# 1e-9 added from a PSUM column, query and key loads two units ahead, first weights converted three units later

## The chip, the cores and the metric

The kernel runs on one core of one Trainium2 chip. The metric is the device time of one execution in microseconds (us). The core has five engines: TensorE (PE in the profile) multiplies matrices into PSUM, VectorE (DVE), ScalarE (ACT) and GpSimd (POOL) work element by element, and SyncE (SP) issues most of the DMAs. Each engine takes its own instructions in order; engines wait for each other by semaphores.

## The reference

Attention with two masks on 8 batches, 8 heads, 576 positions and 64 dimensions, and then a feed-forward layer with 2048 hidden columns:

```python
scores = q @ k^T / sqrt(64)
# heads 0-3: local,   seen where 0 <= row - col < 32
# heads 4-7: strided, seen where col <= row and col % 32 == row % 32
scores = where(mask, scores, -1e9) - max over the row
attn = exp(scores);  attn = attn / (sum(attn) + 1e-9)
x = (attn @ v) as 4608 tokens x 512
h = x @ w_in                # 512 x 2048
out = (h * cos(h)) @ w_out  # 2048 x 512
```

All arrays are fp32 for the user; the weights lie in DRAM as 64-bit numbers.

## The kernel before

**Stages.** The 4608 tokens are 12 blocks of 384. The attention of batches 0 and 1 is done first, alone: this is the opening stage, and all that the change touches. After it the feed-forward layer of blocks 0 and 1 runs, then blocks 2 to 5 with the attention of batches 2 to 7 spread between their steps, then the last six blocks in pairs. From the end of the opening stage on, TensorE has one long list of feed-forward matmuls: `hidden` (L493, the first layer) and `outer` (L519, the second), later L793 and L822. Each fp32 operand is split in a rounded part and a rest (`x_hi`, `x_lo`, and the weights' tiles named `s`).

**Units of the opening stage.** Each batch has seven units of attention, in the order strided, strided, local, strided, strided, local, local: units 0 to 13 for the two batches. A unit goes through these steps:
- SP loads its q and k (tile `qk`, L363 strided, L306 local) and its v (L369, L300).
- TensorE writes the mask into one of three PSUM banks (L239) and adds the scores (L382, L318).
- DVE takes the row maximum (L254) and subtracts it (L255), ACT takes the exponential (L266), DVE sums it (L281), adds 1e-9 (L282, six columns of `z` in SBUF) and takes the reciprocal (L283), and POOL multiplies (L285).
- The result is transposed: strided units by TensorE (L402) and an ACT copy (L406), local ones by DVE (L328).
- TensorE multiplies by v (L416, L347), ACT copies the product out (L424, L430, L355, L356), and ACT and POOL split it in two parts (L447, L448).

**Turns.** A loop over the units (L639) sets the order of TensorE's work by hand; `in_turn` (L200) chains the matmuls. Turn n issues the scores of unit n, then a few *warm matmuls*, then the products of unit n-4, the transposes of unit n-3, and last the softmax of unit n. The warm matmuls (`keep_busy`, L628) multiply a tile of zeros into the PSUM bank `spare` (named `acc2`, rows 0 to 63 of it); nobody uses what they write, they only keep TensorE at work. How many there are is in `BUSY`: 10 ahead of turn 0, then 6, 5, 3, 2, 2, 2 and 1 in each turn after.

**Weights.** `load_weight` (L143) loads a slice f of w_in or w_out (`raw`, L147) and turns it from 64-bit numbers to an fp32 pair: on DVE L161 (for w_out on ACT, L156), L162 and L170, on ACT L169 and L174, on POOL L175. For f = 0 no order to the units was given, and for f = 1 the conversions stand behind the sums (L281) of units 8 and 10 (`SECOND`). A weight's load stands behind the q and k load that `WEIGHTS_AT` names. `need_weights(cv, 1)` is called after the loop (L649), and the other slices follow in the feed-forward steps.

**What else sets the order.** A scheduler orders the instructions of DVE, ACT, POOL and SP within such rules. Where two engines use one PSUM tile, each waits for the other's last use of that tile, whatever columns they use.

Of the kernel before, what the change touches and what calls it, by code (L numbers as in the profile page):

```python
# [19 lines left out]
ALU = mybir.AluOpType  # L20
# [6 lines left out]
P = 128  # L27
# [27 lines left out]

LAG = 3
AHEAD = 2
SECOND = 8, 10
CONVERTED = {3: (1, 0)}

WEIGHTS_AT, WEIGHTS_EACH = 4, 1

PRODUCT_LAG, TRANSPOSE_LAG = 4, 3
BUSY = (10, 6, 5, 3, 2, 2, 2) + 8 * (1,)


KNOTS = ((3, 0), (13, 9), (58, 45))
# [22 lines left out]
def attention_cos_ffn(ctx, tc, qkl, vl, qkvs, w_in, w_out, eye, eye16, mask_l0, mask_l, mask_s, out):  # L90
# [88 lines left out]
    def need_weights(cv, f):  # L179
        nonlocal weights  # L180
        for f in range(weights, f + 1):
            if f < AHEAD:
                after = [summed[n] if f else None for n in SECOND]
            else:
                after = 2 * [reduced[CONVERTED.get(f, (0, f - AHEAD))]]
            load_weight(
                cv, w_in.bitcast(I32)[f], wi_h[f].rearrange("p c n -> p (c n)"),
                wi_l[f].rearrange("p c n -> p (c n)"), after[0], False,
            )
            load_weight(cv, w_out.bitcast(I32)[f], wo_h[f], wo_l[f], after[1], True)  # L190
            weights = f + 1
# [16 lines left out]
    class Attention:  # L208
# [41 lines left out]
        def softmax(self, s, mask, n, w, pn=None):  # L250
            t = self.wk.tile([P, SC], F32, name="t_sb", bufs=3 if self.plain else 2)[:, :n * w].rearrange("p (t w) -> p t w", w=w)
            mx = sm.tile([P, SU], F32, name="mx")
            if self.plain:
                nc.vector.tensor_reduce(out=mx[:, :n], in_=s, op=ALU.max, axis=AX.X)  # L254
                nc.vector.tensor_tensor(  # L255
                    out=t, in0=s, in1=mx[:, :n].unsqueeze(2).broadcast_to([P, n, w]), op=ALU.subtract
                )
            else:
                nc.vector.tensor_tensor(out=t, in0=s, in1=mask, op=ALU.add)
                nc.vector.tensor_reduce(out=mx[:, :n], in_=t, op=ALU.max, axis=AX.X)  # L260
                nc.gpsimd.tensor_tensor(
                    out=t, in0=t, in1=mx[:, :n].unsqueeze(2).broadcast_to([P, n, w]), op=ALU.subtract
                )
            if self.plain:
                e = t
                exps.append(nc.scalar.activation(out=e, in_=t, func=AF.Exp, scale=0.125))  # L266
                if self.copied is not None:
                    order(exps[-1], self.copied, "copies first")
            else:
                e = self.wk.tile([P, SC], F32, name="e_sb", bufs=4)  # L270
                e = e[:, :n * w].rearrange("p (t w) -> p t w", w=w)
                silu = nc.scalar.activation(out=e, in_=t, func=AF.Silu, bias=shift1, scale=0.0625)
                if self.copied is not None:
                    order(silu, self.copied, "copies first")
                nc.scalar.activation(out=t, in_=t, func=AF.Silu, bias=shift2, scale=0.0625)
                nc.vector.scalar_tensor_tensor(
                    out=e, in0=t, scalar=-math.exp(STEP), in1=e, op0=ALU.mult, op1=ALU.add
                )
                nc.scalar.activation(out=e, in_=e, func=AF.Square, scale=math.exp(SHIFT) / STEP)
            z = sm.tile([P, SU], F32, name="z")  # L280
            summed.append(nc.vector.tensor_reduce(out=z[:, :n], in_=e, op=ALU.add, axis=AX.X))  # L281
            nc.vector.tensor_scalar(out=z[:, :n], in0=z[:, :n], scalar1=1e-9, scalar2=None, op0=ALU.add)  # L282
            nc.vector.reciprocal(out=z[:, :n], in_=z[:, :n])  # L283
            pn = e if pn is None else pn
            nc.gpsimd.tensor_tensor(  # L285
                out=pn, in0=e, in1=z[:, :n].unsqueeze(2).broadcast_to([P, n, w]), op=ALU.mult
            )
            return pn
# [7 lines left out]
        def local(self, b, u):  # L296

            def load_v():
                v = self.ld.tile([P, max(VL, VS)], F32, name="v", bufs=5 if self.plain else 3)
                load = nc.sync.dma_start(out=v[:, :VL], in_=vl[b, u])  # L300
                if not self.plain:
                    order(load, tiles[-1], "weights first")
                return v

            qk = self.ld.tile([P, max(QKL, QS + KS)], F32, name="qk")
            loads.append(nc.sync.dma_start(out=qk[:, :QKL], in_=qkl[b, u]))  # L306
            if not self.plain:
                order(loads[-1], tiles[-1], "weights first")
            if self.plain:
                v = load_v()  # L310
            q_t = qk[:, :2 * LQ].rearrange("p (h q) -> p h q", h=2)
            k_t = qk[:, 2 * LQ:QKL].rearrange("p (h k) -> p h k", h=2)
            mask = ml0.rearrange("p (t w) -> p t w", w=KW) if u == 0 else ml.unsqueeze(1).broadcast_to([P, LU, KW])
            s_ps = self.score_bank(mask)

            def score(t, c):
                p, j = divmod(c, 2)
                in_turn(nc.tensor.matmul(  # L318
                    s_ps[quarter_of(c), t * KW:(t + 1) * KW], q_t[half(j), p, QB * t:QB * (t + 1)],
                    k_t[half(j), p, QB * t:QB * t + KW], start=not self.plain, stop=True, skip_group_check=True,  # L320
                ))

            yield [partial(score, t, c) for t in range(LU) for c in range(LH)], "64x32"
            pn = self.softmax(s_ps[:, :LU * KW].rearrange("p (t w) -> p t w", w=KW), mask, LU, KW)

            def turn():
                pt = self.wk.tile([P, LU * KW], F32, name="pt_l")
                nc.vector.transpose(out=pt[:, :LU * KW], in_=pn.rearrange("p t w -> p (t w)"))  # L328
                return pt

            if self.plain:
                pt = turn()
            yield
            if not self.plain:
                pt, v = turn(), load_v()
            v_t = v[:, :VL].rearrange("p (m d) -> p m d", d=D)
            yield
            x_t = [self.wk.tile([P, LQ], F32, name="x_l", bufs=4 if self.plain else 2) for _ in range(2)]
            a_ps = [self.bank(self.products), self.bank(self.transposed)]

            def product(m, c):


                p, j = divmod(c, 2)
                lo, hi = max(m - 1, 0), min(m + 1, LU)
                at = m * KW - QB if m else 0
                in_turn(nc.tensor.matmul(  # L347
                    a_ps[p][half(j), lo * QB:hi * QB], v_t[quarter_of(c), m], pt[quarter_of(c), at:at + (hi - lo) * QB],
                    start=m == turns[0], stop=m == turns[-1], skip_group_check=True,
                ))  # L350


            turns = range(0 if u else 1, LU + 1)
            yield [partial(product, m, c) for m in turns for c in range(LH)], "32x64"
            nc.scalar.copy(out=x_t[1], in_=a_ps[1][:, :LQ])  # L355
            self.copied = nc.scalar.copy(out=x_t[0], in_=a_ps[0][:, :LQ])  # L356
            for p in range(2):
                keep(2 + p, b * S + u * LQ, x_t[p])

        def strided(self, b, p, u):  # L360
# [11 lines left out]
                return v  # L372

            if self.plain:
                v = load_v()
            q_t = qk[:, :QS].rearrange("p (t q) -> p t q", q=GB)
            k_t = qk[:, QS:QS + KS].rearrange("p (t k) -> p t k", k=GB)
            mask = ms.unsqueeze(1).broadcast_to([P, SU, GB])
# [2 lines left out]
            def score(t, i):  # L381
# [6 lines left out]
                partial(score, t, i) for t in range(SU) for i in range(2)  # L388
                if SU * u + t // 2 * 2 + i < NG
            ], "64x64"  # L390
            pn = next(self.pn_s)
            self.softmax(
                s_ps[:, :SU * GB].rearrange("p (t w) -> p t w", w=GB), mask,
# [222 lines left out]
    with ExitStack() as loading:  # L616
        cv = loading.enter_context(tc.tile_pool(name="cv", bufs=3, reuse_waits="tile"))
        with ExitStack() as stack:
# [5 lines left out]
            )  # L624
            units = att.units(0) + att.units(1)
            spare = ps.tile([P, 512], F32, name="acc2")

            def keep_busy(n):  # L628
                for _ in range(n):
                    in_turn(nc.tensor.matmul(  # L630
                        spare[:64], warm, warm.unsqueeze(1).broadcast_to([P, 8, 64]), start=True, stop=True
                    ))

            def run(unit):
# [1 line left out]
                    matmul()  # L636

            keep_busy(BUSY[0])
            for n, unit in enumerate(units):  # L639
                run(unit)  # L640
                if n + 1 < len(BUSY):
                    keep_busy(BUSY[n + 1])
                if n >= PRODUCT_LAG:
                    run(units[n - PRODUCT_LAG])
                    next(units[n - PRODUCT_LAG], None)
                if n >= TRANSPOSE_LAG:
                    next(units[n - TRANSPOSE_LAG])
                next(unit)
# [337 lines left out]
```

## Time and profile before

| | |
|---|---|
| time, median of 3 runs | 917.93 us (916.53 to 918.52) |
| the profiled execution's own time | 917.13 us |
| its span, first to last instruction | 915.3 us |
| mean granted TensorE clock | 0.994 |
| TensorE busy | 898.0 us (98%) |
| DVE, ACT, POOL busy | 524.1, 520.6, 434.2 us |
| opening stage: first score matmul, first `hidden` matmul | 5.82 us, 49.53 us |

How to read it: the profile is of one execution. Rows of the timeline have the start, the busy time, engine and line, the tiles written and read, the form, how often, and in square brackets the idle time of the engine just before with what ended it. PEclk is the clock that TensorE was granted, where 1.00 is full speed; before the first record it is not told. Lines are those of the kernel before, unless the text says that they are of the changed one.

### The profile page before, as it was taken

Reading aid. Unit: us, or ns where it says so; the run is one execution under the profiler, and the core shown is the slowest. Engines: PE = TensorE matmul, PEld = TensorE weight load, DVE = VectorE, ACT = ScalarE, POOL = GpSimd, SP = SyncE. Lnnn points to the kernel's source line nnn. Section 1 sums busy time; section 2 is a strip of 40 time slices with the busy share of each in tenths; the row PEclk is TensorE's granted clock in tenths of the full one; section 3 lists DMA queues with packets and bytes.
Section 4 is the critical chain, followed back from the end, with each engine's and each line's share of the span. In section 5 each row is a group of like instructions: output and inputs, shape, how many; then the busy total and the mean of one; then the engine's idle time right before and its main releaser. Section 6 shows DMA issues by size and latency. Waiting matters only on the chain. (4 is left out here: it accounts for less than half of the span.)

```text
span 915.3 us, 20498 instructions
## 1 busy us (share of the span) xinstructions
PE 898.0 (98%) x7876; PEld 788.2 (86%) x7876; DVE 524.1 (57%) x1018; ACT 520.6 (57%) x1091; POOL 434.2 (47%) x466
## 2 busy tenths in 40 slices
PE   8899999999999999999999999999999999999998
PEld 5589999988888888888888988989998989899987
DVE  5867665446656666666663346556464555544453
ACT  3577776466657665656655445545454545544443
POOL 2756655535665667556745524424433434223231
PEclk9799999999999999999999999999999999999999
DMA  8634325145577867544346855657585655756401
GB/s 305 203 123 158 136 102 183 54 149 169 188 236 264 266 237 229 172 159 152 120 163 192 264 166 184 229 157 233 187 266 190 204 181 186 256 180 196 139 24 69
DMA packets 93408, 166.32 MB, mean 182 GB/s; under 512 B 10752, under 2 KB 34304, under 8 KB 93312
## 3 DMA queue, kind: packets, MB, share of 16 engines
q1 hardware_dynamic: 85248, 157.59, 52.2%
q10 hardware_dynamic: 8064, 7.44, 2.4%
q8 instruction: 62, 1.02, 0.4%
q14 instruction: 34, 0.28, 0.1%
HBM read 125.40 MB, written 39.58 MB: 180 GB/s over the span
## 5 line engine op out<-in xcount | busy, mean ns | idle before, releaser
L808 POOL TENSOR_TENSOR g_lo<-r,g_hi 128x384 fp32r<-128x384 f32 x96 | 99.0, 1031 | 247.9 <-ACT g_hi L807 141.2
L512 POOL TENSOR_TENSOR g_lo<-r,g_hi 128x384 fp32r<-128x384 f32 x94 | 101.4, 1079 | 177.4 <-ACT g_hi L511 99.3
L822 PE MATMUL acc<-s,g_hi 128*128 128x512 f32 x576 | 179.7, 393 | 0.0
L519 PE MATMUL acc<-s,g_hi 128*128 128x512 f32 x564 | 176.2, 396 | 0.0
L519 PEld LDWEIGHTS acc<-s,g_hi 128*128 128x128 f32 x564 | 103.1, 188 | 15.2
L822 PEld LDWEIGHTS acc<-s,g_hi 128*128 128x128 f32 x576 | 106.2, 188 | 10.8
L822 PE MATMUL acc<-s,g_lo 128*128 128x512 f32 x288 | 112.7, 391 | 0.0
L493 PE MATMUL b<-x_hi,s 128*128 128x384 f32 x384 | 108.7, 344 | 1.1 <-POOL s L175 0.8
L802 DVE SCALAR_TENSOR_TENSOR r<-r,h 128x384 f32<-128x384 int32 x96 | 58.2, 607 | 89.4 <-ACT r L801 89.4
L493 PE MATMUL a<-x_hi,s 128*128 128x384 f32 x384 | 108.7, 343 | 0.0
L519 PE MATMUL acc<-s,g_lo 128*128 128x512 f32 x282 | 108.6, 390 | 0.0
L793 PE MATMUL a<-s,s 128*128 128x384 f32 x384 | 83.1, 337 | 0.0
L804 DVE TENSOR_TENSOR r<-r,h 128x384 f32<-128x384 f32 x96 | 69.8, 727 | 22.0 <-ACT r L803 20.7
L803 ACT ACTIVATE r<-r,biases 128x384 f32<-128x384 f32 x96 | 59.2, 617 | 36.7 <-DVE r L802 36.4
L503 ACT ACTIVATE r<-r,biases 128x384 f32<-128x384 f32 x96 | 58.8, 612 | 30.0 <-DVE r L500 28.2
L807 ACT CAST g_hi<-r 128x384 fp32r<-128x384 f32 x96 | 49.2, 512 | 46.0 <-DVE r L804 45.6
L493 PEld LDWEIGHTS b<-x_hi,s 128*128 128x128 f32 x384 | 70.1, 188 | 4.6 <-POOL s L175 1.1
L801 ACT ACTIVATE r<-h 128x384 int32<-128x384 f32 x96 | 50.4, 525 | 39.9 <-DVE h L871 24.5
L793 PEld LDWEIGHTS a<-s,s 128*128 128x128 f32 x384 | 69.4, 188 | 4.2
L493 PEld LDWEIGHTS a<-x_hi,s 128*128 128x128 f32 x384 | 70.2, 188 | 2.6
L511 ACT CAST g_hi<-r 128x384 fp32r<-128x384 f32 x94 | 48.1, 512 | 30.2 <-DVE r L506 27.8
L822 PEld LDWEIGHTS acc<-s,g_lo 128*128 128x128 f32 x288 | 54.1, 188 | 12.4
(149 smaller groups left out, 1774.7 us busy)
## 6 DMA issues: line engine op xcount, KB each, us to landing
s<-wis SPq DMA_DIRECT2D x168, 256.0 KB, 2.9
s<-wos SPq DMA_DIRECT2D x96, 256.0 KB, 3.6
qk<-in_qkvs SPq DMA_DIRECT2D x32, 324.0 KB, 3.7
qk<-in_qkl SPq DMA_DIRECT2D x24, 416.0 KB, 4.2
raw<-in_w_in SPq DMA_DIRECT2D x16, 512.0 KB, 4.2
raw<-in_w_out SPq DMA_DIRECT2D x16, 512.0 KB, 3.4
wos<-s SPq DMA_DIRECT2D x32, 256.0 KB, 4.0
wis<-sr SPq DMA_DIRECT2D x32, 256.0 KB, 2.1
```

The lines of the kernel that those rows point to most:

```text
L493: mm = nc.tensor.matmul(h, w[f][:, c], x[c], start=(i == 0), stop=(i == len(ops) - 1))
L503: sin = nc.scalar.activation(out=r, in_=r, func=AF.Sin, bias=quarter)
L512: chain["rest"] = nc.gpsimd.tensor_tensor(out=g_lo, in0=r, in1=g_hi.bitcast(F32), op=ALU.subtract)
L519: mm = nc.tensor.matmul(acc[t], g[:, ts], w[f], start=(f == 0 and i == 0), stop=(f == NFC - 1 and i == 2))
L793: in_turn(nc.tensor.matmul(bank, w[:, n, c], part, start=start and i == 0, stop=stop and i == len(ops) - 1, skip_group_check=True,))
L801: nc.scalar.activation(out=k, in_=h, func=AF.Copy, scale=1.0 / (2.0 * math.pi), bias=0.25)
L802: nc.vector.scalar_tensor_tensor(out=r, in0=k, scalar=-2.0 * math.pi, in1=h, op0=ALU.mult, op1=ALU.add)
L803: nc.scalar.activation(out=r, in_=r, func=AF.Sin, bias=quarter)
L804: chain["curve"] = nc.vector.tensor_tensor(out=r, in0=r, in1=h, op=ALU.mult)
L807: chain["cast"] = nc.scalar.copy(out=g_hi, in_=r)
L808: chain["rest"] = nc.gpsimd.tensor_tensor(out=g_lo, in0=r, in1=g_hi.bitcast(F32), op=ALU.subtract)
L822: in_turn(nc.tensor.matmul(acc, g[gn][:, ts], w[wn], start=done == 0 and i == 0, stop=done == NFC - 1 and i == 2,))
```

## The change

- **1e-9 from PSUM.** In the opening stage the addition on `z` is no longer a DVE instruction with a constant, but one that adds two tensors: `z` in SBUF and six columns that hold 1e-9. Those columns are columns 448 to 453 of the PSUM bank `spare`, written once by a memset. The warm matmuls write the other 448 columns of the same bank, 448 columns wide in place of 512. Later attention units keep the constant.
- **Loads.** A unit's q and k load is issued two turns ahead of its scores (`LOAD_LEAD`); its v load is issued after its scores. The first weight loads stand behind the q and k load of unit 6 and the following ones (`WEIGHTS_AT` was 4).
- **First weights.** The conversions of w_in and w_out for f = 0 stand behind the sums of units 5 and 6 (`CONVERTED_BEHIND`).
- **Warm matmuls.** 10, then 4, 3, 3, 2, 2, 2 and 1 in each turn after: 34 in place of 38.

```diff
-SECOND = 8, 10
+CONVERTED_BEHIND = ((5, 6), (8, 10))
...
-WEIGHTS_AT, WEIGHTS_EACH = 4, 1
+WEIGHTS_AT, WEIGHTS_EACH = 6, 1
...
-BUSY = (10, 6, 5, 3, 2, 2, 2) + 8 * (1,)
+BUSY = (10, 4, 3, 3, 2, 2, 2) + 8 * (1,)
...
-                after = [summed[n] if f else None for n in SECOND]
+                after = [summed[n] for n in CONVERTED_BEHIND[f]]
...
-            nc.vector.tensor_scalar(out=z[:, :n], in0=z[:, :n], scalar1=1e-9, scalar2=None, op0=ALU.add)
+            if self.plain:
+                nc.vector.tensor_tensor(out=z[:, :n], in0=z[:, :n], in1=self.tiny[:, :n], op=ALU.add)
+            else:
+                nc.vector.tensor_scalar(out=z[:, :n], in0=z[:, :n], scalar1=1e-9, scalar2=None, op0=ALU.add)
...
             if self.plain:
-                v = load_v()
+                yield
...
             yield [partial(score, t, c) for t in range(LU) for c in range(LH)], "64x32"
+            if self.plain:
+                v = load_v()
...
             spare = ps.tile([P, 512], F32, name="acc2")
+            att.tiny = spare[:, 448:448 + SU]
+            nc.vector.memset(att.tiny, 1e-9)
...
-                        spare[:64], warm, warm.unsqueeze(1).broadcast_to([P, 8, 64]), start=True, stop=True
+                        spare[:64, :448], warm, warm.unsqueeze(1).broadcast_to([P, 7, 64]), start=True, stop=True
...
+            for unit in units[:LOAD_LEAD]:
+                next(unit)
             for n, unit in enumerate(units):
+                if n + LOAD_LEAD < len(units):
+                    next(units[n + LOAD_LEAD])
                 run(unit)
```

(The strided units have the same two edits around their v load.) In the changed kernel the addition is L283, the reciprocal L286, the warm matmuls L639, the products L423 and L352, the transposes L409, the scores L387 and L321, ACT's copies L413, L360 and L361, and its casts L454; L161 to L175 and L254 to L281 keep their numbers.

The first place is TensorE's list in turns 6 and 7: the warm matmuls (`acc_215` is the bank `spare`) with what each instruction waits for. Before:

```order
L630 MATMUL acc_215<-warm 64x512
L347 MATMUL acc_515<-pt_l,v 64x64 [waits DVE_49,PE_49]
...
L402 MATMUL acc_547<-ident,pn_s_85 128x128 [waits PE_49,Pool_49]
L402 MATMUL acc_547<-ident,pn_s_85 128x128 x2
L239 LDWEIGHTS ident_69
L239 MATMUL b<-ms,ident_69 128x324
L382 MATMUL b<-qk 54x54 [waits DMAHW4_49]
L382 MATMUL b<-qk 54x54 x11
L630 LDWEIGHTS warm
L630 MATMUL acc_215<-warm 64x512
L416 MATMUL acc_585<-pt,v 64x54 [waits DMAHW3_49,Activation_49]
```

The same stretch in the changed kernel:

```order
L639 MATMUL acc_215<-warm 64x448 [waits DVE_49]
L352 MATMUL acc_514<-pt_l,v 64x64 [waits DMAHW2_49,PE_49]
...
L409 MATMUL acc_546<-ident,pn_s_85 128x128 [waits PE_49,Pool_49]
L409 MATMUL acc_546<-ident,pn_s_85 128x128 x2
L239 LDWEIGHTS ident_69
L239 MATMUL b<-ms,ident_69 128x324
L387 MATMUL b<-qk 54x54 [waits DMAHW2_49]
L387 MATMUL b<-qk 54x54 x11
L639 LDWEIGHTS warm
L639 MATMUL acc_215<-warm 64x448 [waits DVE_49]
L423 MATMUL acc_584<-pt,v 64x54 [waits DMAHW4_49,Activation_49]
```

The matmuls stand in the same order. The first warm matmul of each turn from turn 1 on now waits for DVE: the value that it waits for is that of the addition of the unit before, so in turn 7 that of unit 6.

The second place is ACT's list around the conversions for f = 0 (`t_sb` is a unit's scores, `bits` and `raw` a weight slice). Before, from unit 3's exponential to unit 5's:

```order
L266 ACTIVATE t_sb<-t_sb 128x324 [waits DVE_49]
L156 ACTIVATE bits<-raw 128x512 [waits DMAHW1_49]
L424 COPY x_t<-acc_391 128x6x18x3 [waits PE_49]
L174 CAST s_92<-bits 128x512 [waits DVE_49]
L406 COPY pt<-acc_405 128x324 [waits PE_49]
L266 ACTIVATE t_sb<-t_sb 128x324 [waits DVE_49]
L169 ACTIVATE raw<-raw 128x512 [waits DVE_49]
...
L174 CAST s_124<-bits 128x512 [waits DVE_49]
L266 ACTIVATE t_sb<-t_sb 128x384 [waits DVE_49,Pool_49]
```

The changed kernel, from unit 5's exponential to unit 6's:

```order
L266 ACTIVATE t_sb<-t_sb 128x384 [waits DVE_49,Pool_49]
L454 CAST x_hi<-x_t 128x384 [waits Activation_49]
L454 CAST x_hi<-x_t 128x192
L156 ACTIVATE bits<-raw 128x512 [waits DMAHW3_49]
L169 ACTIVATE raw<-raw 128x512 [waits DMAHW1_49,DVE_49]
L174 CAST s_92<-bits 128x512 [waits DVE_49]
L360 COPY x_l<-acc_515 128x192 [waits PE_49]
L361 COPY x_l<-acc_514 128x192
L454 CAST x_hi<-x_l 128x192 [waits Activation_49]
L454 CAST x_hi<-x_l 128x192
L413 COPY pt<-acc_546 128x324 [waits PE_49]
L266 ACTIVATE t_sb<-t_sb 128x384 [waits Pool_49]
```

The conversion of w_in for f = 0 (L169, and L174 into `s_92`) ended between the exponentials of units 3 and 4 and now stands between those of units 5 and 6; unit 6's exponential is behind its last step.

The third place is the head of SP's list. Before:

```order
L363 DMA qk<-in_qkvs 128x648
L369 DMA v<-in_qkvs 128x384
L363 DMA qk<-in_qkvs 128x648
L369 DMA v<-in_qkvs 128x320
L306 DMA qk<-in_qkl 128x832 [waits DMAHW0_49]
```

The changed kernel:

```order
L368 DMA qk<-in_qkvs 128x648 x2
L309 DMA qk<-in_qkl 128x832
L374 DMA v<-in_qkvs 128x384
L374 DMA v<-in_qkvs 128x320 [waits DMAHW0_49]
L303 DMA v<-in_vl 128x448 [waits DMAHW2_49]
```

Three q and k loads now stand ahead of the first v load.

More of the change, by code (lines that the diff above doesn't have):

```diff
@@ L57 @@
 AHEAD = 2
-SECOND = 8, 10
+CONVERTED_BEHIND = ((5, 6), (8, 10))
 CONVERTED = {3: (1, 0)}
-WEIGHTS_AT, WEIGHTS_EACH = 4, 1
-PRODUCT_LAG, TRANSPOSE_LAG = 4, 3
-BUSY = (10, 6, 5, 3, 2, 2, 2) + 8 * (1,)
+WEIGHTS_AT, WEIGHTS_EACH = 6, 1
+PRODUCT_LAG, TRANSPOSE_LAG, LOAD_LEAD = 4, 3, 2
+BUSY = (10, 4, 3, 3, 2, 2, 2) + 8 * (1,)
 KNOTS = ((3, 0), (13, 9), (58, 45))
@@ L374, in strided @@
             if self.plain:
-                v = load_v()
+                yield
             q_t = qk[:, :QS].rearrange("p (t q) -> p t q", q=GB)
@@ L390, in strided @@
             ], "64x64"
+            if self.plain:
+                v = load_v()
             pn = next(self.pn_s)
```

## The prediction

> **What bounds the kernel now.** I read the busy time in two stretches first, to see where time can be won or lost at all: up to 62 us, and from there on (columns: length, TensorE's busy time, granted clock, DMA share, GB/s).
>
> ```profile
> 0.00:62.00 62.00, 53.68 (x1077) 0.92 0.65 221
> 62.00:915.00 853.00, 844.29 (x6801) 1.00 0.54 179
> ```
>
> From 62 us on TensorE works 844.29 of 853.00 us, on matmuls that the change leaves in their order. So whatever moves the start of that list moves the end by as much, and only the opening stage counts. I read that next in TensorE's timeline: the warm matmuls of turns 1, 3, 6, 7, 10 and 13 (first and last of 13 turns among them), the longest wait, the first `hidden` matmul, its wait for weights, and the first `outer` run.
>
> ```profile
> 8.95 1.27 PE L630 MATMUL acc<-warm 128*64 128x512 bf16 x5
> 12.96 0.62 PE L630 MATMUL acc<-warm 128*64 128x512 bf16 x2
> 20.89 0.40 PE L630 MATMUL acc<-warm 128*64 128x512 bf16 x1
> 25.02 0.40 PE L630 MATMUL acc<-warm 128*64 128x512 bf16 x1
> 32.83 0.40 PE L630 MATMUL acc<-warm 128*64 128x512 bf16 x1
> 37.47 0.88 PE L402 MATMUL acc<-ident,pn_s 128*128 128x128 f32 x3 [2.31 <-ACT x_l L355]
> 47.49 0.40 PE L630 MATMUL acc<-warm 128*64 128x512 bf16 x1
> 49.53 0.42 PE L493 MATMUL a<-x_hi,s 128*128 128x384 f32 x1
> 61.41 0.61 PE L493 MATMUL b<-x_hi,s 128*128 128x384 f32 x2 [0.79 <-POOL s L175]
> 63.27 4.28 PE L519 MATMUL acc<-s,s 128*128 128x512 f32 x18
> ```
>
> The last row begins the feed-forward layer's long list at 63.27 us. The additions of 1e-9 in DVE's timeline, for units 0, 2, 5, 6, 9 and 12 (of 14):
>
> ```profile
> 9.46 0.16 DVE L282 TENSOR_SCALAR z<-z 128x6 f32<-128x6 f32 x1
> 17.09 0.16 DVE L282 TENSOR_SCALAR z<-z 128x6 f32<-128x6 f32 x1
> 25.25 1.14 DVE L282 TENSOR_SCALAR z<-z 128x6 f32<-128x6 f32 x1
> 27.07 0.79 DVE L282 TENSOR_SCALAR z<-z 128x6 f32<-128x6 f32 x1
> 38.59 0.44 DVE L282 TENSOR_SCALAR z<-z 128x6 f32<-128x6 f32 x1
> 48.16 0.32 DVE L282 TENSOR_SCALAR z<-z 128x6 f32<-128x6 f32 x1
> ```
>
> Set one list against the other. TensorE runs its warm matmuls of turn n before the addition of unit n-1 has ended, each time: turn 1 by 0.7 us (8.95 against 9.62), turn 3 by 4.3, turn 6 by 5.5, turn 7 by 2.8, turn 10 by 6.2 and turn 13 by 1.0. Today nobody minds. The stage has slack in both directions, as its idle time and clock show:
>
> ```profile
> 5.80:49.50 43.70, 37.54 (x869) 0.88 0.74 251
> 33.35:36.77 3.42, 1.12 (x56) 0.96 0.09 29
> 36.77:40.18 3.41, 2.71 (x25) 0.50 0.70 233
> 40.18:43.59 3.41, 3.41 (x53) 0.50 0.59 209
> 43.59:47.01 3.42, 3.42 (x81) 0.54 0.47 164
> 47.01:50.42 3.41, 3.36 (x100) 1.00 0.44 133
> ```
>
> TensorE idles 6.2 of the stage's 43.7 us; and after a stretch in which it works only 1.12 of 3.42 us its clock is halved for three such stretches, about 10.2 us.
>
> **The change part by part.**
>
> *The addition loses its lock, and gains a wait.* The 14 additions take 0.16 us where nothing stands in their way, and 6.3 us together:
>
> ```profile
> L282 DVE TENSOR_SCALAR z<-z 128x6 f32<-128x6 f32 x14 | 6.3, 449 | 0.3
> ```
>
> so 6.3 - 14 x 0.16 = 4.1 us are waits inside the instruction. The long ones end with a POOL instruction:
>
> ```profile
> 25.08 1.28 POOL L175 TENSOR_TENSOR s<-bits,s 128x512 fp32r<-128x512 f32 x1
> 26.99 0.84 POOL L285 TENSOR_TENSOR t_sb<-t_sb,z 128x384 f32<-128x384 f32 x1
> ```
>
> (25.25 + 1.14 = 26.39 against 26.36; 27.07 + 0.79 = 27.86 against 27.83). The trace has no addition with an operand in PSUM, so its cost is bounded by the rows: 0.16 us without such a wait, 1.14 with it. I take 0.17, nearest the free one, and keep the other end (4.1 us of DVE time in the stage). The Trainium skill ("SBUF — State Buffer", Who interferes with whom) says that a DVE instruction with at most one SBUF input, outside the 2-port modes, does not contend with GpSimd; by that the 4.1 us go, and by the upper row they stay.
>
> The price is in the order: the first warm matmul of turns 1 to 13 waits for the addition of the unit before, and behind it in TensorE's queue stand that turn's products and transposes and the next turn's scores. (The Trainium skill, "PSUM — Partial Sum Buffer", PSUM bank collisions raise a hardware error, asks that two engines be kept apart by bank and quadrant whatever columns they touch; no row here shows a collision, and by it these waits can't be left out.) TensorE can no longer run ahead. To size this I laid the new order of each engine out in time: every instruction starts when its engine is free and what it waits for has ended, with the durations of the trace's rows. The rows for the longest wait, that of turn 7 (DVE, then ACT, then TensorE; count, total and mean ns in the first two):
>
> ```profile
> L162 DVE SCALAR_TENSOR_TENSOR bits<-raw,bits 128x512 int32<-128x512 int32 x4 | 3.3, 834 | 0.0
> L170 DVE SCALAR_TENSOR_TENSOR bits<-raw,bits 128x512 int32<-128x512 int32 x4 | 2.7, 664 | 0.0
> L281 DVE TENSOR_REDUCE z<-t_sb 128x6 f32<-128x384 f32 x6 | 3.3, 543 | 2.9 <-ACT t_sb L266 2.9
> L161 DVE TENSOR_SCALAR bits<-raw 128x512 int32<-128x512 int32 x2 | 0.8, 422 | 2.0 <-DMA raw<-in_w_in 2.0
> ...
> L266 ACT ACTIVATE t_sb<-t_sb 128x384 f32<-128x384 f32 x6 | 3.2, 526 | 2.8 <-DVE t_sb L255 2.2 <-POOL x_lo L448 0.7
> L406 ACT COPY pt<-acc 128x324 f32<-128x324 f32 x8 | 3.4, 428 | 1.9 <-PE acc L402 1.9
> L169 ACT ACTIVATE raw<-raw 128x512 f32<-128x512 f32 x4 | 2.7, 684 | 4.3 <-DVE bits L162 4.3
> L174 ACT CAST s<-bits 128x512 fp32r<-128x512 f32 x4 | 2.5, 616 | 3.0 <-DVE bits L170 3.0
> L447 ACT CAST x_hi<-x_l 128x192 fp32r<-128x192 f32 x8 | 2.4, 352 | 0.0
> ```
>
> ```profile
> 22.13 0.90 PE L347 MATMUL acc<-pt_l,v 32*64 32x64 f32 x48 [0.83 <-DVE pt_l L328]
> 23.66 0.55 PE L402 MATMUL acc<-ident,pn_s 128*128 128x128 f32 x3 [0.64 <-POOL pn_s L285]
> 24.05 0.30 PE L239 MATMUL b<-ms,ident 128*128 128x324 bf16 x1
> 24.28 0.81 PE L382 MATMUL b<-qk 64*54 64x54 f32 x24
> ```
>
> Turn 6's warm matmul is let go at 24.6 us. TensorE then has some 2.4 us to do (warm 0.2, products 0.9, and from start to start in the last rows transposes 0.4, mask 0.2, scores 0.7) and stands at turn 7's warm matmul at 27.0. That waits for unit 6's sum, this for its exponential, which on ACT stands behind the converted w_in of f = 0: L161 (held by POOL, ends 24.5), L162 (25.3), L169 (26.0), L170 behind unit 6's maximum and subtraction (27.0), L174 (27.8), two copies and two casts of 0.2 to 0.3 each, the copy L413 (29.1), the exponential (29.6), the sum (30.2), L162 for w_out and unit 7's maximum (31.1), the addition (31.3). TensorE stands 4.3 us. All turns, in us:
>
> | turn | 1 | 3 | 4 | 5 | 6 | 7 | 8 | 9 | 10 | 11 | 12 | 13 |
> |---|---|---|---|---|---|---|---|---|---|---|---|---|
> | addition ends | 9.7 | 14.5 | 17.1 | 20.5 | 24.6 | 31.3 | 35.0 | 37.9 | 43.6 | 48.4 | 52.1 | 54.9 |
> | TensorE waits | 1.6 | 1.7 | 1.0 | 0.8 | 2.0 | 4.3 | 1.5 | 1.0 | 3.6 | 2.4 | 1.3 | 0.9 |
>
> Their sum is 22.1. Against it go the 6.2 us that TensorE idles now, 4.8 us of halved clock (half of the 2.71 + 3.41 + 3.42 us of work in those rows) and the smaller warm matmuls below, 1.5: 9.6 us longer. The layout itself puts turn 13's warm matmul at 55.0, `hidden` at 57.0 and `outer` at 70.8, 7.5 us behind the trace's 47.49, 49.53 and 63.27. Laid out likewise, the old order gives 49.1 and 62.9 for the last two, and is up to 1.7 us early in between, so I take 7.5 and keep 9.6.
>
> *Conversions of f = 0 later.* They leave DVE between units 2 and 5 (L161, L162 and L170: 0.4 + 2 x 0.8 + 2 x 0.7 = 3.4 us, and the wait for `raw`) and stand between units 5 and 8. The early turns gain, as turn 3's addition at 14.5 against 17.25 shows; turns 7 and 8 pay. Both are in the table.
>
> *Loads.* None of TensorE's quoted waits ends on a DMA, so earlier q and k gain nothing; the v loads, behind the scores, land before their products four turns later in the layout. Nothing either way; an unknown of 1 us.
>
> *Warm matmuls.* A further one of 512 columns costs (1.27 - 0.40) / 4 = 0.22 us, one of 448 then 0.19. In the turns 28 x 0.22 - 24 x 0.19 = 1.5 us of work goes, and with it some of what keeps the clock up.
>
> *The clock.* Between 26.5 and 29.9 us the layout leaves TensorE some 0.5 us of work, less than the 1.12 that preceded the halved clock. One stretch of 10.2 us at half clock from 29.9 puts `outer` at 72.7, 1.9 later; a second after turn 10's wait of 3.6 us, 3.8 in all. I take 2.8. The Trainium skill ("TensorE: Matmul & The Clock Gate", What's actually happening) has the clock return after one busy window of about 3.4 us; the three rows at 0.50 to 0.54 with TensorE all but fully busy disagree.
>
> **Sum.** 917.13 (the profiled execution; the median lies 0.8 above) + 7.5 + 2.8 = 927.4 us.
>
> **The rivals.**
> - *Faster: the lock was the worse of the two.* Without conversions in the way a loop of two turns is TensorE's 2.4 us and then maximum, subtraction, exponential, sum and addition, 5 x 0.5 = 2.5: 2.5 us a turn against (47.49 - 8.95) / 12 = 3.2 now. If the conversions fall into ACT's and DVE's pauses, the 4.1 us come out: 913. For it speaks that turns 3 to 6 come earlier in the table; against it that the exponential of unit 6 stands behind L174 on ACT. It decides where turn 7 waits under 1 us. Chance 0.09.
> - *No change: the loss is swallowed* by the wait for weights at 61.41. Only 0.8 us can be, and f = 1 is converted behind units 8 and 10 as before, so it moves along. 917 to 918, chance 0.03.
> - *A clock that hardly falls.* A low stretch a third as long costs a third of 1.9: 917.13 + 7.5 + 0.6 = 925.2. Against it stand the three rows. That is what the clock gate's rule, above, would make of it. Chance 0.22.
> - *A clock that stays low.* Each wait of over 2 us may bring the next drop before the last has passed. Halved from 29.9 to 60 us, `outer` comes at 76.2, from 16.3 on at 78.6: 930 to 932.4, say 931. The locked addition's 4.1 us would give as much. Chance 0.20.
>
> **How the numbers follow.** The forecast has 0.46. A measurement of this kernel tells some 0.2% (1.8 us) from no change; all cases but the first two are slower by more: faster 0.09, same 0.03, slower 0.88. The range leaves out those two: from 922.0 (917.13 + 7.5 with a clock that holds, less the 1 us of the loads and the layout's error of up to 1.7) to 934 (the low clock's 932.4 and the same error).
>
> **What would show it.** Right: the first warm matmul of turns 3 to 13 waits for DVE's `z`, 15 us or more together, most at turns 7 and 10; the additions take under 0.2 us; the first `outer` run comes at 71 to 76 us; PEclk is at half in one or more stretches between 25 and 60 us; after it nothing differs. Wrong: waits of TensorE for `z` under 8 us in all, `outer` before 63, or DVE additions still of 1 us.

## The result, and the profile after

| | before | after |
|---|---|---|
| median of 5 runs | 918.52 us (916.53 to 918.91) | 930.63 us (927.89 to 931.45) |
| profiled execution, its own time | 917.13 us | 931.45 us |
| its span | 915.3 us | 929.7 us |
| mean granted TensorE clock | 0.994 | 0.985 |

The ratio is 1.0132 (95% interval 1.0117 to 1.0146): the change makes the kernel 1.3% slower, 12 us by the medians and 14.3 by the two profiled executions. The forecast was 927.4, slower.

To see where, the span is cut in three for each kernel: from 5.80 us to the first `hidden` matmul, from there to the first `outer` run, and the rest (columns: stretch, length, TensorE's busy time, granted clock, DMA share, GB/s). Before:

```profile
5.80:49.53 43.73, 37.57 (x870) 0.88 0.74 251
49.53:63.27 13.74, 12.63 (x207) 1.00 0.35 119
63.27:915.20 851.93, 843.02 (x6793) 1.00 0.54 179
```

After:

```profile
5.80:62.31 56.51, 43.27 (x864) 0.76 0.58 193
62.31:75.93 13.62, 12.60 (x207) 1.00 0.37 120
75.93:929.60 853.67, 843.08 (x6793) 1.00 0.55 179
```

The opening stage is 12.8 us longer, the two steps behind it are not, and the rest is 1.7 us longer. Inside the opening stage TensorE idles 56.51 - 43.27 = 13.2 us in place of 6.2 (+7.1) and is busy 5.7 us longer, although it has fewer and smaller warm matmuls: its clock is 0.76 in place of 0.88. So between these two executions the loss has three parts: 7.1 us of idle time, 5.7 us of slower work, 1.7 us later on. The third is less sure than the others: by the medians the kernel loses 12 us, less than the first two parts together.

What TensorE waits for shows the first part (what waited, for whom: total, times, longest). Up to 75 us:

```profile
PE acc L639 <- DVE z L283: 13.1, 8, 2.9
```

L639 are the warm matmuls, L283 is the addition. Before, no wait of TensorE ended on `z`. TensorE's timeline has the same for turns 1, 3, 6, 7, 8 and 10, and the first `outer` run:

```profile
10.12 0.73 PE L639 MATMUL acc<-warm 128*64 128x448 bf16 x3 [1.45 <-DVE z L283]
15.12 0.54 PE L639 MATMUL acc<-warm 128*64 128x448 bf16 x2 [1.53 <-DVE z L283]
27.23 0.53 PE L639 MATMUL acc<-warm 128*64 128x448 bf16 x1 [1.72 <-DVE z L283]
34.08 0.53 PE L639 MATMUL acc<-warm 128*64 128x448 bf16 x1 [2.90 <-DVE z L283]
38.58 0.53 PE L639 MATMUL acc<-warm 128*64 128x448 bf16 x1
47.62 0.52 PE L639 MATMUL acc<-warm 128*64 128x448 bf16 x1 [2.26 <-DVE z L283]
75.93 2.24 PE L526 MATMUL acc<-s,s 128*128 128x512 f32 x9
```

Read against the additions of units 5, 6, 7 and 9 in DVE's timeline, with the group's row (count, total, mean ns):

```profile
27.03 0.15 DVE L283 TENSOR_TENSOR z<-z,acc 128x6 f32<-128x6 f32 x1
33.88 0.15 DVE L283 TENSOR_TENSOR z<-z,acc 128x6 f32<-128x6 f32 x1
38.37 0.16 DVE L283 TENSOR_TENSOR z<-z,acc 128x6 f32<-128x6 f32 x1
47.40 0.16 DVE L283 TENSOR_TENSOR z<-z,acc 128x6 f32<-128x6 f32 x1
...
L283 DVE TENSOR_TENSOR z<-z,acc 128x6 f32<-128x6 f32 x14 | 2.2, 158 | 0.8
```

The warm matmuls that wait start 0.05 us after the addition of the unit before has ended (27.03 + 0.15 = 27.18, and 27.23). Turn 8's does too (38.37 + 0.16 = 38.53, and 38.58), although no idle time is shown: there TensorE, at half clock, arrives only shortly before. The addition itself is cured: 0.158 us each and 2.2 in all, where it took 6.3, although POOL works at the same time:

```profile
25.82 1.73 POOL L455 TENSOR_TENSOR x_lo<-x_t,x_hi 128x384 fp32r<-128x384 f32 x2 [2.07 <-ACT x_hi L454]
```

The longest wait is the one the prediction named. ACT's timeline ahead of unit 6's exponential (L266, at 31.85) has the converted w_in's last step (L174) in front, and between them four small copies and casts and the copy L413:

```profile
28.14 0.67 ACT L169 ACTIVATE raw<-raw 128x512 f32<-128x512 f32 x1 [1.57 <-DVE bits L162]
29.93 0.62 ACT L174 CAST s<-bits 128x512 fp32r<-128x512 f32 x1 [1.12 <-DVE bits L170]
...
31.53 0.42 ACT L413 COPY pt<-acc 128x324 f32<-128x324 f32 x1
31.85 0.52 ACT L266 ACTIVATE t_sb<-t_sb 128x384 f32<-128x384 f32 x1
```

The second part is the clock. These are windows of 3.41 us, cut where the clock changes (length, TensorE's busy time, clock):

```profile
13.52:16.94 3.42, 1.89 (x30) 1.00 0.83 270
16.94:20.35 3.41, 2.60 (x29) 0.50 0.85 317
20.35:23.76 3.41, 3.41 (x58) 0.50 0.33 96
23.76:27.18 3.42, 1.75 (x69) 1.00 0.89 288
27.18:30.59 3.41, 3.36 (x61) 0.50 0.45 159
30.59:34.01 3.42, 0.59 (x22) 1.00 0.85 298
34.01:37.42 3.41, 3.34 (x35) 0.50 0.40 125
37.42:40.83 3.41, 3.29 (x46) 0.50 0.56 187
40.83:44.24 3.41, 3.41 (x105) 0.50 0.53 171
44.24:47.66 3.42, 1.16 (x34) 1.00 0.43 142
47.66:51.07 3.41, 3.41 (x67) 0.50 0.65 236
51.07:54.48 3.41, 1.75 (x45) 1.00 0.11 38
54.48:57.89 3.41, 3.41 (x63) 0.50 0.63 210
```

Before, cut in the same way:

```profile
33.06:36.47 3.41, 1.41 (x57) 1.00 0.13 45
36.47:39.89 3.42, 2.42 (x25) 0.50 0.64 211
39.89:43.30 3.41, 3.41 (x42) 0.50 0.59 206
43.30:46.71 3.41, 3.41 (x73) 0.50 0.53 187
```

The waits leave windows with 0.59 to 1.89 us of work, and the window behind each has half the clock. The clock is at half in five stretches, 27.3 us in all, with 26.2 us of work in them; before there was one stretch of 10.2 us, with 9.2 us of work. What half the clock costs is shown by the same 48 score matmuls of a local unit, at half clock and at full:

```profile
21.25 1.51 PE L321 MATMUL acc<-qk 64*32 64x64 f32 x48
24.64 0.88 PE L321 MATMUL a<-qk 64*32 64x64 f32 x48
```

At full clock they take 0.58 of the time. An estimate from these rows: 0.42 x (26.2 - 9.2) = 7.1 us of slower work, less 1.5 us for the smaller warm matmuls (the prediction's figure), is 5.6 of the measured 5.7.

The third part is in the attention that runs between the later feed-forward steps: TensorE's transposes wait for ACT's copy of `x_l`. Before (L402, from 76 us on) and after (L409):

```profile
PE acc L402 <- ACT x_l L355: 3.7, 5, 1.2
```

```profile
PE acc L409 <- ACT x_l L360: 5.4, 7, 1.2
```

### The profile page after: what moved, and what is told of

It is laid out like the page before. It is cut to its first block, busy times and chain, and to the rows that moved or that the text cites. A ratio compares the mean times of both kernels' runs of the same rounds, so it can differ in the third digit from the quotient of the medians.

```text
span 929.7 us, 20497 instructions
## 1 busy us (share of the span) xinstructions
PE 903.5 (97%) x7872; PEld 793.6 (85%) x7872; DVE 523.7 (56%) x1019; ACT 520.4 (56%) x1091; POOL 433.6 (47%) x466
## 5 line engine op out<-in xcount | busy, mean ns | idle before, releaser
L526 PEld LDWEIGHTS acc<-s,g_hi 128*128 128x128 f32 x564 | 103.2, 188 | 15.1
L518 ACT CAST g_hi<-r 128x384 fp32r<-128x384 f32 x94 | 48.1, 511 | 29.6 <-DVE r L513 27.3
```

The source lines that it names most:

```text
L526: mm = nc.tensor.matmul(acc[t], g[:, ts], w[f], start=(f == 0 and i == 0), stop=(f == NFC - 1 and i == 2))
```

## The experiments

Theory one is the prediction's: TensorE's warm matmuls and DVE's additions share a PSUM bank, so that TensorE waits for each addition. Its rivals: the later conversions and loads are what costs; the smaller number of warm matmuls lets the clock fall; an addition of two tensors is itself the cost. Beside each result stands the first `outer` run's start (63.27 us before, 75.93 after) and the *tail*, the span less that start (852.0 and 853.8). The first four kernels ran on one chip, and so did the next four and the last four; each ratio is to runs of the kernel before there.

**The column in PSUM alone** (kernel before, with the addition from PSUM and warm matmuls of 448 columns):

```diff
-            nc.vector.tensor_scalar(out=z[:, :n], in0=z[:, :n], scalar1=1e-9, scalar2=None, op0=ALU.add)
+            if self.plain:
+                nc.vector.tensor_tensor(out=z[:, :n], in0=z[:, :n], in1=self.tiny[:, :n], op=ALU.add)
...
+            att.tiny = spare[:, 448:448 + SU]
```

> The kernel before with the PSUM addition alone (warm matmuls 448 columns wide, as many as before; loads and conversions as before). Theory 1, the shared bank: the warm matmul of each turn waits for the addition of the unit before, so nearly the whole loss comes back: first outer run 7 us later at full clock and 10 to 13 later with halved clock, 926 to 931 us, TensorE waiting over 12 us for DVE's z. Theory 2, the later conversions and the loads cost the time: within 2 us of before. Theory 3, fewer warm matmuls let the clock fall: within 2 us of before, since their number stays.

927.41 us, ratio 1.0100 (1.0083 to 1.0117). TensorE's waits up to 75 us, and the first `outer` run:

```profile
PE acc L635 <- DVE z L283: 14.3, 10, 4.1
```

```profile
75.18 3.15 PE L522 MATMUL acc<-s,s 128*128 128x512 f32 x13
```

This edit alone brings the waits for `z` (L635 are its warm matmuls) and moves the first `outer` run by 11.9 of the 12.7 us. By the medians it brings 9.2 of the 12.1 us, since its tail is 849.7.

**The rest without it** (the changed kernel, with the addition of the constant):

```diff
-            if self.plain:
-                nc.vector.tensor_tensor(out=z[:, :n], in0=z[:, :n], in1=self.tiny[:, :n], op=ALU.add)
-            else:
-                nc.vector.tensor_scalar(out=z[:, :n], in0=z[:, :n], scalar1=1e-9, scalar2=None, op0=ALU.add)
+            nc.vector.tensor_scalar(out=z[:, :n], in0=z[:, :n], scalar1=1e-9, scalar2=None, op0=ALU.add)
```

> The changed kernel with the addition of a constant as before, and nothing in the bank of the warm matmuls. Theory 1: no wait of TensorE for z, the additions up to 1.2 us long again, outer at 62 to 63 us, 916 to 918.5 us: the rest of the change is worth nothing or up to 1 us. Theory 2: stays at 927 or above. Theory 3: the clock is halved for more than 10 us with 34 small warm matmuls, 920 to 927.

918.10 us, ratio 0.9994 (0.9984 to 1.0004), `outer` at 62.91. Later conversions, earlier loads and fewer warm matmuls cost nothing together. That rival falls, for as long as TensorE need not wait for additions.

**The changed kernel without warm matmuls behind turn 0** (turns count from 0, as in the sections above; some of the expectations count them from 1):

```diff
-BUSY = (10, 4, 3, 3, 2, 2, 2) + 8 * (1,)
+BUSY = (10, 4)
```

> The changed kernel with the PSUM addition, but no warm matmuls after turn 0, so that nothing writes the bank of 1e-9 any more. Theory 1: TensorE waits for z nowhere; outer at 63 us if the clock holds, up to 72 if it stays halved: 917 to 926 us, below the changed kernel either way. Theory 2: 927 or above. Theory 3: the clock falls further than in the changed kernel, 931 or above.

914.99 us, ratio 0.9964 (0.9951 to 0.9977): 16 us faster than the changed kernel by the medians, and faster than the kernel before. The additions still read PSUM; with nobody else in the bank no wait for `z` is left, and the first `outer` run is at 62.30. No theory expected so low a time: theory one's lower end was 917. The rival that fewer warm matmuls cost time through the clock falls: the clock was at half for 13.7 us in the opening stage, against 10.2 in the kernel before and 17.1 in the kernel with the constant and all 34 warm matmuls, and neither version of the changed kernel is slower than the kernel before.

**What the locked addition was worth** (changed kernel without any addition of 1e-9 in the opening stage):

```diff
-            if self.plain:
-                nc.vector.tensor_tensor(out=z[:, :n], in0=z[:, :n], in1=self.tiny[:, :n], op=ALU.add)
-            else:
+            if not self.plain:
```

> The changed kernel with the addition of 1e-9 left out of the opening stage (part of the computation is left out: 14 instructions of DVE). Theory 1: neither lock nor wait, outer at 60 to 62 us, 914.5 to 917: what the lock of the 14 additions cost shows here, some 2 us. Theory 2: 927 or above. Theory 3: 920 or above.

917.23 us, ratio 0.9988 (0.9979 to 0.9997), `outer` at 62.44. Without the whole addition, 6.3 us of DVE time, the kernel gains about 1 us on the kernel before (0.3 to 1.9 by the interval): this is the most that the change could have won by it, and it was expected to be more.

**The kernel before without its warm matmuls behind turn 0** (22 are left out, where the expectation counts 27), and the same **with the column in PSUM:**

```diff
-BUSY = (10, 6, 5, 3, 2, 2, 2) + 8 * (1,)
+BUSY = (10, 6)
```

> The kernel before without the 27 warm matmuls of turns 2 to 14 (it keeps the 10 ahead of the attention and the 6 of turn 1), with the addition of a constant and with the old loads and conversions. No value that is given out depends on them. Theory A, the 3 us that the changed kernel won without its warm matmuls come from the warm matmuls alone, which occupy TensorE and hold up nothing useful but what is behind them: 27 x 0.22 = 6 us of work go, about half of it on the path: 914 to 916, first outer run at 60 to 61.5 us. Theory B, they come from the addition that no longer waits for POOL (operand in PSUM): no change here, 917.5 to 919, outer at 62.3 to 63.3. Theory C, the old purpose of the warm matmuls, TensorE's clock: at half for one stretch of 10 us more, 920 to 923, outer at 65 to 68.

> The kernel before with the column in PSUM added, and without the warm matmuls of turns 2 to 14; loads and conversions as before. The shared bank then has no writer that waits for an addition but in turn 1. Theory A, warm matmuls alone: the same as the kernel before without them, within 1 us (914 to 916). Theory B, the addition's lock: 914.5 to 916 while the kernel before without warm matmuls stays at 917.5 or more. Both: 2 us or more below it. In each case TensorE's waits for z are under 1 us in all, additions 0.16 us each, and the first outer run is at 60 to 62.5 us. If the reading of the shared bank were wrong and the PSUM operand costs by itself: 922 or more.

915.40 us, ratio 0.9969 (0.9956 to 0.9982), and 914.32 us, ratio 0.9966 (0.9954 to 0.9978). So the 3 us go with leaving out the warm matmuls, and the addition's form adds nothing that can be told. These two and the third experiment are the fastest kernels of this study, equal within their intervals. The place of the gain was expected wrongly: the first `outer` run is at 63.19 and 62.54, hardly earlier, while the tails are 849.2 and 849.9. A tail as short stands also in kernels that keep their warm matmuls (849.7 with the column alone), so why leaving them out wins is open. They do bear on the clock: without them the kernel before has it at half for 17.1 us in place of 10.2, as theory C said in kind, but its price of 2 us or more does not appear.

**Warm matmuls in the early turns alone** (changed kernel; turns 0 to 5 keep theirs):

```diff
-BUSY = (10, 4, 3, 3, 2, 2, 2) + 8 * (1,)
+BUSY = (10, 4, 3, 3, 2, 2, 2)
```

> The changed kernel with warm matmuls up to turn 6 alone (those of turns 7 to 14, one each, left out; nothing given out depends on them). Theory one, each shared-bank wait is a delay of its own that adds up over the turns: what remains are the waits of turns 1 to 6, 5 to 7 us in all; laid out in time the first outer run comes at 67.5 us at full clock, 3.3 before that of the changed kernel's layout; with the clock at half for 10 to 17 us of the stage (2 to 4 us more) 69 to 72, time 922 to 926. Rival, the loss is that of one long wait (turn 7, behind the conversions of f = 0) and the early waits are made up later: 916 to 919, outer at 62 to 65. Rival, the loss is the clock's alone, which falls after the first waits: as slow as the changed kernel, 929 to 931.

919.39 us, ratio 1.0019 (1.0006 to 1.0032), less than theory one's 922. TensorE's waits up to 76 us, then the first `outer` run:

```profile
PE acc L423 <- ACT pt L413: 6.4, 4, 4.3
PE acc L639 <- DVE z L283: 4.5, 4, 1.5
```

```profile
67.81 4.28 PE L526 MATMUL acc<-s,s 128*128 128x512 f32 x18
```

The early turns leave 5.5 us in the opening stage against the kernel without warm matmuls there (67.81 - 62.30), and the late turns bring the other 8.1 (75.93 - 67.81): the loss adds up over the turns. The rival by which the early waits are made up later asked for 62 to 65; theory one's 69 to 72 was too late, although the clock was at half for 13.7 us, as it said; its waits for `z` were 5 to 7 us and measured 4.5. The time is near that rival's all the same, since the tail is 848.9 here. The row on `pt` shows a second thing: in turn 7 the products stand behind the same conversions on ACT, and with the warm matmul gone TensorE waits 4.3 us there for the copy L413.

**The column in SBUF** (kernel before; 24 bytes a partition for the column):

```diff
+            att.tiny = const.tile([P, SU], F32, name="tiny")
+            nc.vector.memset(att.tiny, 1e-9)
```

> The kernel before with the addition's second operand a column of 1e-9 in SBUF, in place of the constant (and nothing in PSUM; warm matmuls of 512 columns as before). Theory one, the loss comes from the bank: no wait of TensorE for z, first outer run at 62 to 64 us, 917 to 919, no different from before. The rival that an addition of two tensors is itself the cost: 922 or more. On the lock: if the operand in PSUM is what frees the addition from POOL, the 14 additions still take 3 to 7 us in all here, some of them over 0.8; if any addition of two tensors is free, 14 x 0.16 = 2.3 us.

924.05 us, ratio 1.0064 (1.0048 to 1.0081), and yet no wait for `z`, and the first `outer` run at 62.41: the opening stage is as before. No theory expected a loss where it is: the tail is 858.0 us. On the lock the group's row is plain:

```profile
L283 DVE TENSOR_TENSOR z<-z,tiny 128x6 f32<-128x6 f32 x14 | 6.2, 443 | 0.3
```

With both operands in SBUF the addition is as slow as with the constant, with one in PSUM it takes 158 ns. It is the place of the operand that frees it, not the form.

**The column in SBUF, 64 bytes wide**, and **the 24 bytes allocated and filled, but not added:**

```diff
-            att.tiny = const.tile([P, SU], F32, name="tiny")
+            att.tiny = const.tile([P, 16], F32, name="tiny")
```

> The kernel before that adds a column in SBUF, with a tile of 64 bytes a partition for the column in place of 24 (the other 40 unused). With 24 bytes the opening stage was unchanged (first outer run at 62.41 us), but the matmuls after it took 395 to 398 ns where they took 390 to 396, and the end came 5 us later. Theory one, the 24 bytes moved the tiles that lie behind them off an alignment that TensorE's reads like: with 64 bytes 917 to 919, the stretch behind the first outer run back at 849 to 853 us. Rival, the addition of two tensors itself slows what follows: 922 to 925 again. On the lock nothing changes: the 14 additions 5 to 7 us in all, 6.2 with 24 bytes.

> The kernel before with the 24-byte column in SBUF allocated and filled, but not added: the additions take the constant as before. Theory one, the place of the tiles behind it is what costs: 922 to 925, matmuls behind the first outer run 395 to 398 ns, the stretch behind it 856 to 859 us. Rival, the addition with two operands in SBUF costs: 917 to 919, that stretch 849 to 853 us.

921.85 us, ratio 1.0047 (1.0029 to 1.0065), and 923.82 us, ratio 1.0064 (1.0046 to 1.0081); tails 858.2 and 859.0. So the addition is not the cause, since the unused column costs as much, and 64 bytes do not mend it, against the expectation. (The profiled execution with 64 bytes is 3.1 us above its median, so its tail overstates the loss.) What is longer are TensorE's matmuls. Groups of the kernel before (count, total us, mean ns):

```profile
L822 PE MATMUL acc<-s,g_lo 128*128 128x512 f32 x288 | 112.7, 391 | 0.0
...
L519 PE MATMUL acc<-s,g_lo 128*128 128x512 f32 x282 | 108.6, 390 | 0.0
```

The same with the unused column:

```profile
L824 PE MATMUL acc<-s,g_lo 128*128 128x512 f32 x288 | 113.9, 396 | 0.0
...
L519 PE MATMUL acc<-s,g_lo 128*128 128x512 f32 x282 | 110.5, 397 | 0.0
```

That is 5 and 7 ns a matmul. That the allocation moves the tiles behind it is the likely reason, but no run shows a tile's address; which property of it would do this stays open.

**Twice the warm matmuls in turns** (changed kernel), to part waits and clock:

```diff
-BUSY = (10, 4, 3, 3, 2, 2, 2) + 8 * (1,)
+BUSY = (10, 8, 6, 6, 4, 4, 4) + 8 * (2,)
```

> The changed kernel with twice the warm matmuls in turns 1 to 14 (4 3 3 2 2 2 then 8 times 1 become 8 6 6 4 4 4 then 8 times 2; 24 more of 0.19 us, 4.6 us of work that no output depends on). It is to part the loss into the waits and the clock. Laid out at full clock the first outer run comes at 74.3 us, 3.5 behind the changed kernel's layout; the changed kernel came 5.1 behind its own layout with 27 us at half clock. Theory one, a window of little work brings the half clock, and twice the warm matmuls lift TensorE's work in the windows before: 7 to 17 us at half clock, outer at 75.5 to 77.5, 929 to 933, waits for z 11 to 15 us. Rival, the waits alone set the low clock, whatever runs between them: again some 27 us at half, outer at 79 to 80.5, 933 to 936. Rival, the clock was no cost, but the waits: full clock or not, outer at 74 to 75.

927.96 us, ratio 1.0110 (1.0091 to 1.0129); waits for `z` 12.5 us, first `outer` run at 76.73, and two stretches at half clock:

```profile
28.14:41.80 13.66, 11.20 (x150) 0.50 0.51 169
48.62:58.86 10.24, 8.97 (x122) 0.50 0.36 120
```

4.6 us more work moves the first `outer` run by 0.8 only (76.73 against 75.93), inside theory one's 75.5 to 77.5. The waits for `z` are as long as before; what pays is the clock: 11.20 + 8.97 = 20.2 us of work were done at half clock, 6.0 less than in the changed kernel, which by the 0.42 above is some 2.5 us won (an estimate). So waits and clock are two costs, as theory one has it, though the clock stayed at half for 23.9 us, not for 7 to 17. The time is below theory one's 929 to 933 and the changed kernel's median, which is the tail's doing (848.6).

**The first conversions as before** (changed kernel):

```diff
-CONVERTED_BEHIND = ((5, 6), (8, 10))
+SECOND = 8, 10
...
-                after = [summed[n] for n in CONVERTED_BEHIND[f]]
+                after = [summed[n] if f else None for n in SECOND]
```

> The changed kernel with the conversions of f = 0 as before (w_in as soon as it has landed, w_out behind unit 8's or 10's sum as in the kernel before); column in PSUM, loads and warm matmuls as changed. Theory one, the waits only move: in the layout turns 4 to 6 wait 2.3, 3.3 and 1.4 us in place of 1.0, 0.8 and 2.0, turn 7 waits 1.9 in place of 4.3, and the first outer run is at 70.9 us as against 70.8: no different from the changed kernel within 3 us, 927 to 932, longest wait ahead of turn 7. Rival, the later conversions are what costs, once an addition holds TensorE: 3 to 5 us faster than the changed kernel, 925 to 927, outer at 71 to 73.

927.55 us, ratio 1.0101 (1.0084 to 1.0118); waits for `z` 13.5 us, `outer` at 74.15. The loss stays: 10.9 of the 12.7 us are there with the conversions where they were. The waits only move, as theory one has it; the 1.8 us between the two first `outer` runs are within its 3. The longest wait is not at turn 7, as it said, but at turn 4 (2.5 us). By the ratios the two kernels differ by 2.8 us, with intervals that just overlap, and the tail has the rest (851.7 against 853.8), so some 3 us are the most that the later conversions can be charged with here.

## Why the prediction was right, and where its sizes were off

**Only the opening stage counts.** Nearly: 12.7 of the 14.4 us by which the span grew. The statement that nothing differs behind the first `outer` run was wrong by 1.7 us in these two executions: the waits for `x_l` went from 3.7 to 5.4. Among the kernels with the tiles of the kernel before in their places the tail was between 848.6 and 853.8 us, and the sum of these waits between 2.1 and 5.4; what sets them was not found. Most of the 3 us that the kernels without warm matmuls win belongs to the same open question.

**The addition's lock.** Right to the tenth: 6.3 - 2.2 = 4.1 us gone, 0.158 taken as 0.17. The rule that was quoted for it (the Trainium skill, "SBUF — State Buffer", Who interferes with whom) is borne out by the run with the column in PSUM (158 ns). The run with it in SBUF (443 ns) has two SBUF inputs. The constant (449 ns) has one, so by that rule it would have run in a 2-port mode, which no row here shows. The rival *the lock was the worse of the two* had a fair price for DVE's time and a wrong one for the kernel's: leaving the addition out altogether gave 1 us.

**The waits.** The mechanism is shown: with the column alone the loss is there, without it, or without the other user of the bank, it is gone. Turn 7's wait was named with its cause and is the longest (2.9 us; 4.3 forecast), turn 10 the second (2.26; 3.6 forecast). The sum was mis-sized: 13.1 us in place of 22.1, under the 15 that were set as a mark. The forecast table, at full clock, against the trace (an addition's end is its start and duration):

| turn | 3 | 4 | 5 | 6 | 7 | 8 | 9 | 10 | 13 |
|---|---|---|---|---|---|---|---|---|---|
| addition ends, forecast | 14.5 | 17.1 | 20.5 | 24.6 | 31.3 | 35.0 | 37.9 | 43.6 | 54.9 |
| addition ends, trace | 15.1 | 17.8 | 22.6 | 27.2 | 34.0 | 38.5 | 42.1 | 47.6 | 60.3 |

The lag grows from 0.6 us to 2.1 in the first half-clock stretch (16.94 to 23.76) and to 5.4 at the end. Slow work and waiting fill the same time: at half clock TensorE arrives later at the additions, so that turns 5, 8 and 9 show no idle time where 0.8, 1.5 and 1.0 us were forecast. With 22.1 us of waits TensorE would have idled 22.1 - 6.2 = 15.9 us more; it idled 7.1 us more and worked 5.7 us longer. The total came out nearer than these parts, because what slow work takes is no longer waited, and that trade was not in the prediction: in this the nearness of the total was luck.

**The clock.** This is the term of the sum that failed in size: 2.8 us were taken for one stretch at half clock, or at most two; there were five, 27.3 us. The layout's 70.8 us at full clock against the measured 75.93 makes it 5.1. Laid out again with the five measured stretches it gives 76.7, 0.8 past the trace; the column alone, laid out with its own three (27.3 us), gives 74.7 for a measured 75.18. These are calculations: no run has the waits at full clock, so the 7.5 and the 5.1 were not measured apart. With them the sum for the profiled execution is 917.1 + 7.5 + 5.1 + 1.7 = 931.4. What was missed is the first stretch, which begins at 16.94, behind turn 3's wait of 1.53 us and ahead of the long ones, and that the drop follows thin windows and not the longest two waits alone. Half clock was priced as half of the work; the two rows on L321 show 0.42. That the clock drops so often is the rival *a clock that stays low* in half: it drops again and again, but it also comes back between.

On this the prediction said that before's three rows disagree with the Trainium skill's rule of one busy window ("TensorE: Matmul & The Clock Gate", What's actually happening). Its rows were not cut where the clock changes; cut there, the first of them has 2.42 us of work and is no busy window, and one row disagrees: the one at 39.89, busy throughout and followed by half clock. After, three of the five stretches last one window of 3.41 us (27.18, 47.66 and 54.48), as the rule has it, and the other two end with the first window that is wholly busy (2.60, then 3.41 us of work; 3.34, 3.29, then 3.41).

**Conversions, loads, warm matmuls.** Without the waits they are nothing together (ratio 0.9994); turn 3's addition came early as said (15.1 against 17.25 before). That fewer warm matmuls take some of what keeps the clock up was left without a price. The kernel with the constant and all three has the clock at half for 17.1 us in place of 10.2, so it may well be so, but the time does not show it; why is open.

## What to carry to other kernels

Ask of every operand that moves to PSUM who else writes that bank: a filler that nobody reads becomes the work that everybody waits for, and here an in-order queue turned 0.16 us additions into 13 us of waiting. A wait of TensorE is priced twice where it thins a window so that the next one runs at half clock, so count the thin windows and not the longest wait. Before hastening an operation, leave it out once: here that shows 1 us to be won, and leaving out the warm matmuls showed 3, for a reason that stays open.

## What the hardware showed beyond that

**Thin windows.** In all fourteen profiles, from 5 to 70 us, every full-clock window of 3.41 us with 1.81 us of TensorE work or less was followed by one at half clock, and every one with 2.10 us or more by one at full clock; between them both occur. The kernel with early warm matmuls shows it at the extreme:

```profile
26.66:30.07 3.41, 0.18 (x6) 1.00 0.45 152
30.07:33.48 3.41, 3.41 (x48) 0.50 0.69 234
```

The emptiest window still has the full clock: the price falls on the one behind it.

**24 bytes that nobody reads** made the whole kernel 0.64% slower, probably by moving the tiles behind them in SBUF; a trial that allocates something is compared with one that only allocates it.
